# A bank of products goes from two engines to VectorE alone, and one load moves up Pool's queue

## The chip, the cores and the metric

The kernel runs on one core of one Trainium2 chip. The metric is the device time of one execution in microseconds. A core has five engines that run side by side, each through its own instructions in program order: TensorE (matrix products into PSUM), VectorE, ScalarE, Pool (GpSimd) and SyncE, which here only issues transfers. Sixteen DMA engines move the data that SyncE, Pool and, at the end, ScalarE ask for.

## The reference

Two layers stand one behind the other: a global filter in the frequency domain, then a feed-forward net.

```python
# x: (8, 3008, 256); filt_r, filt_i: (1505, 256)
X = np.fft.rfft(x, axis=1)
Y = X * (filt_r + 1j * filt_i)[None, :, :]
y = np.fft.irfft(Y, n=3008, axis=1)
# tokens: 8 * 3008 = 24064; w_in: (256, 2048); w_out: (2048, 256)
h = y.reshape(24064, 256) @ w_in
g = np.maximum(0.01 * h, h)
out = g @ w_out
```

## The kernel before

The transform of 3008 points is split as 94 x 32 and done with matrix products in fp16. For each batch there are four stages on TensorE: stage 1 (94 points; `s1`), stage 2 (32 points with the twiddle factors; `s2`), whose result is multiplied by the filter, and the two inverse stages (`sa` and `sb`). Between stages the data must be turned round. For batches 1 to 7 this goes through DRAM: SyncE stores (`dz1`, `dz2`, lines 259 and 329) and reloads (lines 266 and 273). The result stands in `yt`, and from there the net takes chunks of 512 tokens, 47 in all: `moe1` (line 516) makes `h` in two wide PSUM tiles and ScalarE writes `g`; the second layer follows one chunk later, in the first three chunks by plain products with `w_out` (`plain`, line 641) and later by a scheme of seven products (line 580).

Everything is issued in a fixed order. For batches 1 to 7 and the net, a planner puts each step at a due time on one time line and hands the steps out in that order. For batch 0 the order is written by hand, in the string `FIRST`. Batch 0 is turned round on VectorE (`t1`, `t2`), and nothing of the net can begin before it is through. A step of `FIRST` is a name and its arguments; `hf` is a half of the 256 channels, `c` the first column of the frequency index, `n` the number of columns, `i` the real or the imaginary part, `b` the bank:

- `s2p hf c n i b`: the matmuls of stage 2 for `n` columns, into bank b0 to b2 (512 wide: `pf0` to `pf2`) or b3, b4 (1024 wide: `ph0`, `ph1`).
- `s2d hf c n i`: VectorE multiplies the whole bank by the filter and writes `prods` (line 400, in `times_filter`).
- `s2a hf c n i`: ScalarE copies four columns of a bank to one of six `spare` tiles in SBUF (line 417); `s2m hf c 4 i`: Pool multiplies that copy by the filter (line 400).
- `s2h hf c n i`: VectorE multiplies four columns of a bank whose other four go through ScalarE and Pool.
- `sap`, `sae`: the first inverse stage and its evacuation by ScalarE (lines 427 and 430); `sap hf c b` needs the products of its four columns for both `i`.
- `t2`, `sbp`, `sbe`: turning, the last stage, and its evacuation to `yt`.
- `x 0`, `x 1`: Pool issues the loads of the first and the second half of batch 1's input (line 191; each 768 KB as it lands, cast from fp32 to fp16 on the way); `w_out`: Pool issues the load of the second layer's weights (line 463; 1024 KB as it lands, cast too).

Pool computes and issues loads through one queue, in order. The loads that it has issued before, for batch 0, the filter, the constants and `w_in`, go through the same DMA queue.

The part of batch 1's work in the planner that matters here: its 16 stage-1 groups (line 254) are put between the first layer's products from the start of the net on, their results go to `dz1` in eight stores by SyncE (line 259), four reloads follow (line 266), and then stage 2 (line 303). The second layer's first product stands behind the first layer's 16 steps of chunk 0.

Of the kernel before, what the change touches and what calls it, by code (L numbers as in the profile page):

```python
# [75 lines left out]
def kernel(  # L76
# [9 lines left out]
    nc = tc.nc  # L86
    B, N, D = x.shape
# [264 lines left out]
    act, dve = nc.scalar.copy, nc.vector.tensor_copy  # L352
# [6 lines left out]
    held, spare = {}, [scrp.tile([P, 4, DH], FP32, tag=f"p{i // 2 + 1}", name=f"spare{i}") for i in range(6)]  # L359
# [39 lines left out]
    def times_filter(eng, hf, c, n, i, x):  # L399
        eng.tensor_tensor(prods[hf][:, i, ds(c, n), :], x, fa_sb[:, ds(c, n), ts(hf, DH)], AL.mult)  # L400
# [1 line left out]
    def s2d(hf, c, n, i):  # L402
        times_filter(nc.vector, hf, c, n, i, held.pop(("s2", hf, c, i)))

    def four_of(hf, c, n, i):

        at_c = c if ("s2", hf, c, i) in held else c - 4
        key = ("s2", hf, at_c, i)
        return (held.pop(key) if c - at_c == n - 4 else held[key])[:, ds(c - at_c, 4), :]

    def s2h(hf, c, n, i):
        times_filter(nc.vector, hf, c, 4, i, four_of(hf, c, n, i))

    def s2a(hf, c, n, i):

        held["xf", hf, c, i] = xf = spare.pop(0)
        act(xf[:], four_of(hf, c, n, i))

    def s2m(hf, c, n, i):
        xf = held.pop(("xf", hf, c, i))  # L420
# [44 lines left out]
    def round_x(n0, n, e):  # L465
# [10 lines left out]
        s2a 1 16 8 0, s2p 0 4 4 0 b1, s2p 1 16 8 1 b3, s2d 0 4 4 0, s2a 1 20 8 0, sap 0 8 b2, s2d 0 4 4 1,  # L476
        s2a 1 16 8 1, s2a 1 20 8 1, s2m 0 12 4 0, s2p 0 16 8 1 b4, sap 0 0 b1, s2p 1 0 8 1 b3, s2m 0 12 4 1,
        sap 0 12 b0, s2m 1 20 8 0, sae 0 8 A, s2d 0 16 8 1, sae 0 0 A, s2p 1 8 8 1 b4, sap 0 4 b2, s2d 1 0 8 1,
        sap 0 16 b1, sae 0 12 A, s2p 1 8 8 0 b3, sap 0 20 b0, s2a 1 8 8 1, s2h 1 12 8 1, s2m 1 20 8 1,
        s2m 1 8 8 1, sae 0 4 A, s2d 1 8 8 0, s2p 1 0 8 0 b4, sae 0 16 A, sap 1 20 b2, s2d 1 0 8 0, sap 1 12 b1,  # L480
        sae 0 20 A, sap 1 8 b0, s2m 1 16 8 0, sae 1 20 A, s2m 1 16 8 1, x 0, x 1, w_out, sae 1 12 A, sae 1 8 A,
        sap 1 16 b3, sae 1 16 A, sap 1 4 b2, t2 1, sae 1 4 A, sap 1 0 b4, t2 0, sae 1 0 A, warm 4, sbp 0 1 b1,
        sbp 0 4 b0, sbp 0 0 b3, sbp 0 3 b2, t2 3, sbe 0 1 A, sbe 0 4 A, sbe 0 0 A, sbp 0 2 b4, sbp 0 7 b1,
        sbp 0 6 b0, t2 2, sbe 0 2 A, sbe 0 7 A, sbp 0 5 b3, sbp 1 0 b4, sbp 1 1 b1, sbe 0 6 A, sbe 0 5 A,
        sbe 1 1 A, sbe 0 3 D, sbe 1 0 D
    """
    steps = dict(s1p=s1p, s1e=s1e, t1=t1, s2p=s2p, s2d=s2d, s2h=s2h, s2a=s2a, s2m=s2m, sap=sap, sae=sae, t2=t2,
                 sbp=sbp, sbe=sbe, x=load_x, w_out=load_w_out, xc=round_x, warm=keep_warm)
    for step in FIRST.split(","):
        what, *args = step.split()  # L490
# [210 lines left out]
    while queue:  # L701
        time, n, stage, b, g, f = heapq.heappop(queue)
# [62 lines left out]
```

## Time and profile before

| what | before |
|---|---|
| three runs, us | 752.94, 753.91, 754.14 (median 753.91) |
| the profiled execution, us | 754.14 |
| its span, first to last instruction, us | 752.3 |
| mean granted clock of TensorE | 0.996 |
| busy: TensorE, ScalarE, VectorE, Pool | 98%, 74%, 66%, 22% |
| DMA: mean over the span | 151 GB/s |
| DMA share in the windows 22:28 us, 28:30 us, 30:50 us | 0.95 to 1.11, 0.38 and 0.08, 0.53 to 1.39 |

The span is the time from the first to the last instruction that the profiler recorded; what lies around it is 1.84 us. A row of a group of instructions names the line, the engine, the operation, the tiles written and read, how often, busy time and the mean of one. "Idle before" is the time that an engine stood still before an instruction, with what ended it. A DMA share of 1.00 means that on average all sixteen engines were busy; it can read over 1. The granted clock of TensorE is a share of its full speed.

### The profile page before, as it was taken

To read this page: it belongs to the slowest core of one execution; us is meant where nothing else is said; L and a number is where in the kernel's file an instruction comes from. 1 tells how busy PE (TensorE), PEld (TensorE's weight loads), DVE (VectorE), ACT (ScalarE), POOL (GpSimd) and SP (SyncE) were. 2 spreads that over 40 slices of the span, in tenths; PEclk is the share of its full clock that TensorE was granted. 3 is DMA by queue.
4 is the path that set the end of the run, shared out by engine and by line. 5 is a ranking of instruction groups with operands and counts; after the bars stand their busy time and mean duration, and the time that the engine had idled before them with its cause. 6 is when DMAs were issued, how large, how long until landed. Compare 5 with 4: busy or idle time off the path is not lost.

```text
span 752.3 us, 19411 instructions
## 1 busy us (share of the span) xinstructions
PE 740.2 (98%) x8017; PEld 529.1 (70%) x8017; DVE 498.9 (66%) x684; ACT 559.8 (74%) x756; POOL 169.1 (22%) x172
## 2 busy tenths in 40 slices
PE   9989999999999999999999999999999999999997
PEld 3546667767777777877678777787777777777776
DVE  6867555677767766667667766776677676465565
ACT  4755797788887777787778777877777777767662
POOL 6602430342222321221133222212212210000000
PEclk9999999999999999999999999999999999999999
DMA  9996798887886568565676566544454333211012
GB/s 204 201 226 178 167 216 233 211 184 194 223 204 160 138 180 214 132 155 148 184 185 166 151 171 169 139 135 127 141 163 122 106 100 103 61 54 54 29 47 67
DMA packets 119560, 113.64 MB, mean 151 GB/s; under 512 B 16352, under 2 KB 92768, under 8 KB 119280
## 3 DMA queue, kind: packets, MB, share of 16 engines
q1 hardware_dynamic: 104128, 94.66, 42.8%
q0 software_dynamic: 15056, 17.49, 16.0%
q8 instruction: 62, 1.02, 0.6%
q10 hardware_dynamic: 288, 0.26, 0.1%
q14 instruction: 26, 0.21, 0.1%
HBM read 57.51 MB, written 50.33 MB: 143 GB/s over the span
## 4 chain that ended last, share of the span: by engine, by line
PE 89%; DMA 7%; POOL 1%; DVE 1%; issue 1%; ACT 0%; SPq 0%; POOLq 0%; DVEq 0%; ACTq 0%
PE ph L516 41%; PE po_ps L580 18%; PE pf L580 18%; PE pf L254 3%; PE pf L346 3%; DMA w_out_sb<-in_moe_w_out_dram 3%; PE pf L303 2%; PE pf L325 2%; PE po_ps L641 1%; PE pf L641 1%; DMA f_sb<-fwd_const 1%; DMA fa_sb<-in_filt_i_dram 1%; DMA p_b_g<-p_b_g 1%; DMA dz<-big 1%; POOL prod L400 1%
## 5 line engine op out<-in xcount | busy, mean ns | idle before, releaser
L521 ACT ACTIVATE gt_c<-ph 128x1024 f16<-128x1024 f32 x376 | 385.6, 1026 | 139.7 <-PE ph L516 129.0
L516 PE MATMUL ph<-yt,w_in_sb 128*128 128x512 f16 (+7 forms) x1728 | 447.8, 352 | 0.2
L580 PEld LDWEIGHTS <-gt_c 128*128 128x128 f16 x2800 | 202.2, 98 | 91.3 <-issue 0.2
L318 POOL TENSOR_TENSOR y_b_g<-p_b_g,p_b_g 128x512 f16<-128x512 f32 x84 | 118.1, 1407 | 418.8 <-DMA p_b_g<-p_b_g 219.1
L580 PEld LDWEIGHTS <-big 128*128 128x128 f16 x2128 | 151.3, 98 | 61.6 <-issue 0.2
L516 PEld LDWEIGHTS <-w_in_sb 128*128 128x128 f16 x1728 | 137.6, 98 | 20.0 <-issue 0.5
L312 DVE TENSOR_TENSOR p_b_g<-pf,fb_sb 128x512 f32<-128x512 f32 x78 | 53.7, 689 | 32.6 <-PE pf L303 19.4
L580 PE MATMUL po_ps<-wt_sb,gt_c 128*128 128x128 f16 x704 | 70.0, 219 | 0.0
L580 PE MATMUL pf<-wt_sb,gt_c 128*128 128x128 f16 x688 | 68.4, 219 | 0.0
L580 PE MATMUL pf<-w_out_sb,gt_c 128*128 128x128 f16 x720 | 67.9, 219 | 0.0
L580 PE MATMUL po_ps<-wt_sb,big 128*128 128x128 f16 x720 | 67.4, 219 | 0.0
L580 PE MATMUL pf<-wt_sb,big 128*128 128x128 f16 x704 | 67.2, 219 | 0.0
L580 PE MATMUL po_ps<-w_out_sb,gt_c 128*128 128x128 f16 x688 | 66.0, 219 | 0.0
L257 ACT CAST big<-pf 128x512 f16<-128x512 f32 x98 | 57.1, 588 | 11.9 <-PE pf L254 10.5
L336 ACT CAST yt<-pf 128x376 f16<-128x376 f32 x120 | 56.3, 472 | 10.8 <-PE pf L346 7.9
L315 DVE TENSOR_TENSOR p_b_g<-pf,fa_sb 128x512 f32<-128x512 f32 x84 | 57.3, 682 | 0.2
L553 DVE TENSOR_TENSOR big<-gt_c 128x2048 f16<-128x2048 f16 (+1 forms) x46 | 56.8, 1236 | 0.1
L553 DVE TENSOR_TENSOR big<-big,gt_c 128x2048 f16<-128x2048 f16 (+1 forms) x45 | 55.2, 1226 | 0.1
L553 DVE TENSOR_TENSOR gt_c<-gt_c 128x2048 f16<-128x2048 f16 x43 | 54.4, 1266 | 1.0
L553 DVE TENSOR_TENSOR big<-gt_c,big 128x2048 f16<-128x2048 f16 (+1 forms) x45 | 54.1, 1202 | 0.0
L327 ACT CAST big<-pf 128x512 f16<-128x512 f32 x84 | 49.0, 584 | 4.9 <-PE pf L325 3.0
L254 PE MATMUL pf<-x_sb,small_sb 94*128 94x512 f16 x109 | 41.8, 384 | 0.1
(91 smaller groups left out, 625.8 us busy)
## 6 DMA issues: line engine op xcount, KB each, us to landing
dz<-big SPq DMA_DIRECT2D x98, 256.0 KB
p_b_g<-p_b_g SPq DMA_DIRECT2D x156, 128.0 KB
out_dram<-ost_c_h SPq DMA_DIRECT2D x118, 128.0 KB
big<-dz SPq DMA_DIRECT2D x42, 256.0 KB
big<-dz SPq DMA_DIRECT2D x56, 192.0 KB
x_sb<-in_x_dram POOLq DMA_DIRECT2D x40, 192.0 KB, 4.5
x_sb<-in_x_dram POOLq DMA_DIRECT2D x2, 768.0 KB, 8.2
w_in_sb<-in_moe_w_in_dram POOLq DMA_DIRECT2D x1, 1024.0 KB, 13.1
```

The costliest lines, as they stand in the source:

```text
L254: nc.tensor.matmul(ps, fwd1[:N1], x_sb[:N1, ds(2 * g, 2), :], start=True, stop=True)
L257: copy(st[:, ds(2 * (g % 2), 2), :], ps)
L312: nc.vector.tensor_tensor(p2[:], ps, fb, AL.mult)
L315: nc.vector.tensor_tensor(p1[:], ps, fa, AL.mult)
L318: ("y", b, g), lambda: nc.gpsimd.tensor_tensor(y1[:], p1[:], p3[:], AL.add)))
L327: nc.scalar.copy(st2[h % 4][:, ds(2 * (g % 2), 2), :], ps)
L336: copy(yv, ps.rearrange("p c a -> p a c"))
L346: nc.tensor.matmul(ps[:, j, :], z2[h % 4][:K4, j, ts(dt, P)], i1_sb[:K4, 4 * h + j, :], start=True, stop=True)
L516: nc.tensor.matmul(ph[:, j, ds(t - ci * CH, e - t)], w_in_sb[:, dt, ts(ct, P)], yt[:, dt, ds(t % N, e - t)], start=(dt == 0), stop=(dt == ...
L521: nc.scalar.activation(gts[ci][:, ds(2 * g, 2), :], ph, AF.Lrelu)
L553: nc.vector.tensor_tensor(*(v[:, ds(c0, n)] for v in (o, i0, i1)), op)
L580: nc.tensor.matmul(po[:, t], a()[:, c, ts(t, P)], w[:, c, :], start=(c == 0), stop=(c == NCH - 1))
```

## The change

In `FIRST`, the eight columns 8 to 15 of half 1, part 1 (bank b4) were split: columns 8 to 11 went through ScalarE and Pool (`s2a 1 8 8 1`, `s2m 1 8 8 1`), and VectorE took columns 12 to 15 (`s2h 1 12 8 1`). After the change VectorE takes the whole bank (`s2d 1 8 8 1`), in the same place of its queue. The step `s2h`, now without use, and its helper are taken out. Further, `x 0` is written before `s2m 1 16 8 0`, and `x 1` and `w_out` stay behind `s2m 1 16 8 1`; on Pool's queue the issue of `x 0` thus stands ahead of the last two products and no longer behind them. All the rest of the string is the same, with line breaks moved.

```diff
-    def four_of(hf, c, n, i):
-
-        at_c = c if ("s2", hf, c, i) in held else c - 4
-        key = ("s2", hf, at_c, i)
-        return (held.pop(key) if c - at_c == n - 4 else held[key])[:, ds(c - at_c, 4), :]
-
-    def s2h(hf, c, n, i):
-        times_filter(nc.vector, hf, c, 4, i, four_of(hf, c, n, i))
-
     def s2a(hf, c, n, i):
 
+        at_c = c if ("s2", hf, c, i) in held else c - 4
         held["xf", hf, c, i] = xf = spare.pop(0)
-        act(xf[:], four_of(hf, c, n, i))
+        key = ("s2", hf, at_c, i)
+        act(xf[:], (held.pop(key) if c - at_c == n - 4 else held[key])[:, ds(c - at_c, 4), :])
...
-        sap 0 16 b1, sae 0 12 A, s2p 1 8 8 0 b3, sap 0 20 b0, s2a 1 8 8 1, s2h 1 12 8 1, s2m 1 20 8 1,
-        s2m 1 8 8 1, sae 0 4 A, s2d 1 8 8 0, s2p 1 0 8 0 b4, sae 0 16 A, sap 1 20 b2, s2d 1 0 8 0, sap 1 12 b1,
-        sae 0 20 A, sap 1 8 b0, s2m 1 16 8 0, sae 1 20 A, s2m 1 16 8 1, x 0, x 1, w_out, sae 1 12 A, sae 1 8 A,
+        sap 0 16 b1, sae 0 12 A, s2p 1 8 8 0 b3, sap 0 20 b0, s2d 1 8 8 1, s2m 1 20 8 1, sae 0 4 A,
+        s2d 1 8 8 0, s2p 1 0 8 0 b4, sae 0 16 A, sap 1 20 b2, s2d 1 0 8 0, sap 1 12 b1, sae 0 20 A, sap 1 8 b0,
+        x 0, s2m 1 16 8 0, sae 1 20 A, s2m 1 16 8 1, x 1, w_out, sae 1 12 A, sae 1 8 A, sap 1 16 b3,
```

More of the change, by code (lines that the diff above doesn't have):

```diff
@@ L403, in s2d, with s2a @@
         times_filter(nc.vector, hf, c, n, i, held.pop(("s2", hf, c, i)))
-    def four_of(hf, c, n, i):
+    def s2a(hf, c, n, i):
         at_c = c if ("s2", hf, c, i) in held else c - 4
+        held["xf", hf, c, i] = xf = spare.pop(0)
         key = ("s2", hf, at_c, i)
-        return (held.pop(key) if c - at_c == n - 4 else held[key])[:, ds(c - at_c, 4), :]
-    def s2h(hf, c, n, i):
-        times_filter(nc.vector, hf, c, 4, i, four_of(hf, c, n, i))
-    def s2a(hf, c, n, i):
-        held["xf", hf, c, i] = xf = spare.pop(0)
-        act(xf[:], four_of(hf, c, n, i))
+        act(xf[:], (held.pop(key) if c - at_c == n - 4 else held[key])[:, ds(c - at_c, 4), :])
     def s2m(hf, c, n, i):
@@ L478 @@
         sap 0 12 b0, s2m 1 20 8 0, sae 0 8 A, s2d 0 16 8 1, sae 0 0 A, s2p 1 8 8 1 b4, sap 0 4 b2, s2d 1 0 8 1,
-        sap 0 16 b1, sae 0 12 A, s2p 1 8 8 0 b3, sap 0 20 b0, s2a 1 8 8 1, s2h 1 12 8 1, s2m 1 20 8 1,
-        s2m 1 8 8 1, sae 0 4 A, s2d 1 8 8 0, s2p 1 0 8 0 b4, sae 0 16 A, sap 1 20 b2, s2d 1 0 8 0, sap 1 12 b1,
-        sae 0 20 A, sap 1 8 b0, s2m 1 16 8 0, sae 1 20 A, s2m 1 16 8 1, x 0, x 1, w_out, sae 1 12 A, sae 1 8 A,
[L482 to L485, printed above, removed]
+        sap 0 16 b1, sae 0 12 A, s2p 1 8 8 0 b3, sap 0 20 b0, s2d 1 8 8 1, s2m 1 20 8 1, sae 0 4 A,
+        s2d 1 8 8 0, s2p 1 0 8 0 b4, sae 0 16 A, sap 1 20 b2, s2d 1 0 8 0, sap 1 12 b1, sae 0 20 A, sap 1 8 b0,
+        x 0, s2m 1 16 8 0, sae 1 20 A, s2m 1 16 8 1, x 1, w_out, sae 1 12 A, sae 1 8 A, sap 1 16 b3,
+        sae 1 16 A, sap 1 4 b2, t2 1, sae 1 4 A, sap 1 0 b4, t2 0, sae 1 0 A, warm 4, sbp 0 1 b1, sbp 0 4 b0,
+        sbp 0 0 b3, sbp 0 3 b2, t2 3, sbe 0 1 A, sbe 0 4 A, sbe 0 0 A, sbp 0 2 b4, sbp 0 7 b1, sbp 0 6 b0,
+        t2 2, sbe 0 2 A, sbe 0 7 A, sbp 0 5 b3, sbp 1 0 b4, sbp 1 1 b1, sbe 0 6 A, sbe 0 5 A, sbe 1 1 A,
+        sbe 0 3 D, sbe 1 0 D
     """
-    steps = dict(s1p=s1p, s1e=s1e, t1=t1, s2p=s2p, s2d=s2d, s2h=s2h, s2a=s2a, s2m=s2m, sap=sap, sae=sae, t2=t2,
+    steps = dict(s1p=s1p, s1e=s1e, t1=t1, s2p=s2p, s2d=s2d, s2a=s2a, s2m=s2m, sap=sap, sae=sae, t2=t2,
                  sbp=sbp, sbe=sbe, x=load_x, w_out=load_w_out, xc=round_x, warm=keep_warm)
```

## The prediction

> **What bounds the kernel now.** I read the page first, then TensorE's waits, then the chain of work that ended last over the first 60 us, then Pool and VectorE in order of time, then one-microsecond windows.
>
> ```profile
> span 752.3 us, 19411 instructions
> ...
> PE 740.2 (98%) x8017; PEld 529.1 (70%) x8017; DVE 498.9 (66%) x684; ACT 559.8 (74%) x756; POOL 169.1 (22%) x172
> ```
>
> TensorE is busy 740.2 of 752.3 us. So a change is worth what it does to TensorE's few idle microseconds, or to its clock. The waits of TensorE in the first 75 us (us in total, times, longest):
>
> ```profile
> PE po_ps L641 <- DMA w_out_sb<-in_moe_w_out_dram: 3.3, 1, 3.3
> ...
> PE pf L303 <- DVE p_b_g L315: 0.9, 1, 0.9
> ...
> PE ph L427 <- POOL prod L400: 0.2, 1, 0.2
> ```
>
> The largest wait of the kernel is the first product of the second layer (L641) waiting for its weights. The chain of waits says why they are late (start, length, what):
>
> ```profile
> 26.80 2.28 POOL prod L400 x2
> 29.08 1.06 POOL x_sb L191 x2
> 30.14 18.87 DMA w_out_sb<-in_moe_w_out_dram
> 49.01 0.05 issue
> 49.05 0.61 PE po_ps L641 x4
> ```
>
> Pool issues the load of `w_out` only after its products and the two loads of batch 1's `x`; it lands 18.87 us later. TensorE's last matmul before it ended at 45.79 (49.05 less the 3.26 us of idle that the timeline gives). Pool, then VectorE, in order of time:
>
> ```profile
> 23.04 2.29 POOL L400 TENSOR_TENSOR prod<-spare,fa_sb 128x512 f16<-128x512 f32 x2 [0.55 <-DMA fa_sb<-in_filt_i_dram]
> 25.68 3.40 POOL L400 TENSOR_TENSOR prod<-spare,fa_sb 128x512 f16<-128x512 f32 x3 [0.35 <-ACT spare L417]
> 29.02 1.13 POOL L191 DMA_DIRECT2D x_sb<-in_x_dram  x2
> ```
>
> ```profile
> 22.82 2.35 DVE L400 TENSOR_TENSOR prod<-ph,fa_sb 128x1024 f16<-128x1024 f32 x2
> 25.64 3.11 DVE L400 TENSOR_TENSOR prod<-ph,fa_sb 128x512 f16<-128x512 f32 x3 [0.46 <-ACT spare L417]
> 28.66 2.36 DVE L436 STREAM_TRANSPOSE big<-big 128x1024 f32<-128x1024 f32 x2
> ```
>
> Windows (the last three figures are granted clock, DMA share, GB/s):
>
> ```profile
> 28.00:29.00 1.00, 0.93 (x5) 0.29 (x4) 1.00 (x2) 1.00 (x3) 1.00 (x1) 1.00 0.38 74
> 29.00:30.00 1.00, 0.87 (x5) 0.39 (x5) 1.00 (x2) 0.88 (x2) 1.00 (x3) 1.00 0.08 20
> 34.00:35.00 1.00, 0.82 (x13) 0.47 (x9) 0.55 (x1) 0.81 (x3) 0.00 (x0) 1.00 0.99 205
> 47.00:48.00 1.00, 0.00 (x0) 0.00 (x0) 0.00 (x0) 0.00 (x0) 0.00 (x0) 1.00 1.11 290
> 51.00:52.00 1.00, 1.00 (x11) 0.55 (x10) 0.00 (x0) 1.00 (x2) 0.00 (x0) 0.50 1.13 344
> ```
>
> Three things are to be seen. At 29 to 30 the DMA engines are nearly idle, though 2.6 MB of loads are about to be asked for. At 47 all five engines stand still. At 51 TensorE runs at half clock: the half-microsecond windows show 0.72 at 50.0, 0.50 from 50.5 to 53.5, 0.87 at 53.5, then 1.00. So the wait costs twice: 3.26 us idle, and 0.5 x (0.28 + 6 x 0.50 + 0.13) = 1.70 us of lost clock.
>
> **The change, part by part.** Four columns of one bank change hands: ScalarE loses one copy (`s2a 1 8 8 1`), Pool one product (`s2m 1 8 8 1`), VectorE's 512-wide product becomes 1024 wide, and on Pool's queue the issue of `x 0` moves ahead of the last two products. The instruction orders of TensorE and SyncE are the same; only the wait of one matmul (`sap 1 8`) on Pool goes.
>
> *VectorE.* Now the 512-wide product starts 0.46 us late, because ScalarE still reads the same bank, and 3.11 us later all three are done. Without the copy it starts when VectorE is free, at about 25.18 (22.82 + 2.35). The bank is full by then, TensorE's last of its matmuls being at 24.94. Three products at the pitch of the row (2.35 / 2 = 1.17) end at 28.69 instead of 28.66: +0.03, nothing. If that 0.46 had not been there, the extra 1.17 - 0.62 = 0.55 would have shown in the transposes.
>
> *ScalarE* loses 0.59 us at 25.02; TensorE runs back to back there, so I count nothing. *TensorE:* the 0.2 us wait for Pool goes, since Pool ends its last product earlier (below). ScalarE's last evacuation (now 30.54 to 31.16) then ends some 0.2 earlier, and the third transpose, which waits 0.16 for it, starts at about 31.08 instead of 31.19. The first layer starts 0.11 earlier.
>
> *Pool.* From 25.33, the end of the second row: one issue of x (1.13 / 2, at most the 0.60 of the dearer one) to 25.93, two products (2 x 1.13) to 28.20, the other issue (0.53) to 28.73, then `w_out`: 1.41 earlier than 30.14. Each x issue is one DMA of 768 KB; the waits of `x 0` (VectorE's cast, stage-1 matmuls) were met by 13 us. Behind it wait two products, which end at 28.20 instead of 29.08, so nobody is later.
>
> *When `w_out` lands.* Late bound: only the issue shift counts, 49.01 - 1.41 = 47.60. Early bound: transfers in this queue follow one another, and there is a hole to fill. The bytes before `x 0` are through at about 28.4 (DMA share 0.38 in the window 28 to 29); x's first bytes come at 30.0. In the windows from 30.0 to 38.6 1.58 MB moved, the two halves of x; so `w_out` began at 38.6, and 1.05 MB to about 48.5 is 106 kB/us, beside SyncE's stores and a load from 37.6 on. With `x 0` asked for at 25.33 its bytes follow at 28.4: 1.57 MB at 205 kB/us end at 36.1. SyncE's first store is issued at 37.59, so `w_out` runs alone to about 38.2 (430 kB), then 619 kB at 106 kB/us: 44.0, and 0.5 to landing, 44.5. The two bounds are 44.5 and 47.6; I take 44.5, because its rows are this very queue.
>
> That is 1.3 us ahead of 45.7, when TensorE asks. So the stall goes: 3.26. The clock loss follows the stall; after the 0.95 us wait at 70 us the clock stays 1.00, so without a stall I count 1.70 back. Bounds of the clock part: 0 to 1.70.
>
> *A rule that speaks against the move.* Pool's issue at 38.37 took 0.90 where the one before took 0.52, and ended at 39.27, just after VectorE's L674, fp16 in SBUF, which ran from 38.20 to 39.16. The Trainium skill ("SBUF — State Buffer", on the "DVE blocks DMA" trap) says that Pool cannot write descriptors while VectorE runs a two-port mode; if that took hold of the new place until 28.69, `x 0` would be out at 29.3 and `w_out` at 32.1, and the sum would stay at 754.1. The same page says that an operation with one operand in SBUF does not contend, and here the products of both engines ran side by side at 1.13 and 1.17. I cost the new place at 0.57 us, the row of the same issue, and nothing more.
>
> *The sum.* 0.11 + 3.26 + 1.70 = 5.07. The profiled execution took 754.14 with a span of 752.3, 1.84 around it: 749.07. That execution is the slowest of the three, 0.23 above the median 753.91, so 748.8 to 749.1 is meant; I say 748.9. Does the rest keep it? After 49 us TensorE's idle is below 2 us up to the tail, and SyncE's stores and reloads are tied to TensorE's own progress, so they move along.
>
> **The rivals.**
> *Part of the wait stays.* `w_out` lands at 47.60: the stall is 1.85 instead of 3.26 and the early start of the layer is lost in it. With the clock kept 754.14 - 1.41 - 1.70 = 751.0; with the clock lost as now 752.7. For it: SyncE's queue competes with an unknown share. Against: the hole at 28.4 to 30. The row is that 3.26 us of idle halves the clock and 0.95 does not. The Trainium skill ("TensorE: Matmul & The Clock Gate", Part 1) says that it takes an idle window of about 3.4 us, free-running; the 3.26 here is already shorter, and by that rule 1.85 would give the 751.0.
>
> *Nothing moves.* The queue is bound by bytes and not by issues, and the hole is only landing time: `w_out` at 49.0, 754.1. Against: 20 GB/s at 29 to 30.
>
> *The debt comes due at batch 1's reload: slower.* TensorE's first L303 (64.72) would come at 59.65. Its operand is loaded by SyncE's L266, issued at 60.63 and used 4.09 later, after eight stores (L259), the last issued at 55.80. DMA is full until 54.3. If the backlog still ends there and the last store then takes 6.03 us, as this queue's p_b_g transfer on the chain at 194.09 does, the operand is there at 54.3 + 6.03 + 4.09 = 64.4: a stall of 4.8, and 1.70 of clock again, 749.07 + 6.5 = 755.5 or more. It decides against the change from 63.0 on (59.65 + 5.07 - 1.70). For it: DMA is saturated from 38 to 54. Against: share 0.03 at 55 to 56, so the backlog ends before the last store, and it ends sooner when the hole is filled.
>
> **How the numbers follow.** Stall gone, 748.9: 0.67. Part stays, clock kept, 751.0: 0.14; clock lost, 752.7: 0.06. Nothing moves, 754.1: 0.03. Slower, 755.5: 0.10. About 0.2%, 1.5 us, is what a measurement can tell here. Faster: 0.67 + 0.14 = 0.81; same: 0.06 + 0.03 = 0.09; slower: 0.10. The range goes from 747.8 (the lowest of the runs lies 1.0 under the median, and the front may give 0.1) to 751.5 (the second case and half a microsecond); 0.19 is left out.
>
> **What will show it.** `x 0` issued at about 25.4, `w_out` at 28.7, no DMA hole at 28 to 30; `w_out` landed by 45; TensorE busy through 45 to 50 at clock 1.00; three 1024-wide VectorE products ending at 28.7; the first L303 at about 59.7 without a wait. It is wrong if `w_out` lands after 46, or if another wait of some microseconds appears between 50 and 70.

## The result

The changed kernel takes 748.94 us (median of four runs, 748.77 to 749.92), the kernel before beside it 754.02 (752.94 to 754.99): the ratio is 0.9936, with a 95% interval of 0.9918 to 0.9953. The profiled execution took 749.05 with a span of 747.3; the one before had 754.14 and 752.3.

The page of the changed kernel, its first lines:

```profile
span 747.3 us, 19408 instructions
...
PE 738.1 (99%) x8017; PEld 528.8 (71%) x8017; DVE 504.8 (68%) x684; ACT 559.2 (75%) x755; POOL 165.0 (22%) x171
```

TensorE's busy time fell by 2.1 us and the span by 5.0, with 8017 matmuls both times: what went is idle time and slow matmuls, not work. Pool in order of time (start, length, engine, line, what):

```profile
22.91 2.28 POOL L400 TENSOR_TENSOR prod<-spare,fa_sb 128x512 f16<-128x512 f32 x2 [0.48 <-DMA fa_sb<-in_filt_i_dram]
25.13 0.60 POOL L191 DMA_DIRECT2D x_sb<-in_x_dram  x1
25.75 2.29 POOL L400 TENSOR_TENSOR prod<-spare,fa_sb 128x512 f16<-128x512 f32 x2
27.98 0.57 POOL L191 DMA_DIRECT2D x_sb<-in_x_dram  x1
28.55 1.18 POOL L456 DMA_DIRECT2D w_out_sb<-in_moe_w_out_dram  x1
```

`x 0` is issued at 25.13 and `w_out` at 28.55; the trace gives 14.8 us to the landing of `w_out`, 43.35, where it was 49.01. The same windows as before (the last three figures are granted clock, DMA share, GB/s):

```profile
28.00:29.00 1.00, 1.00 (x5) 0.44 (x6) 1.00 (x2) 0.99 (x2) 1.00 (x3) 1.00 1.16 238
29.00:30.00 1.00, 1.00 (x6) 0.49 (x5) 1.00 (x2) 1.00 (x3) 0.73 (x1) 1.00 1.00 209
34.00:35.00 1.00, 0.77 (x15) 0.46 (x12) 0.63 (x2) 0.95 (x3) 0.00 (x0) 1.00 1.05 221
47.00:48.00 1.00, 1.00 (x14) 0.65 (x13) 0.09 (x1) 1.00 (x2) 0.00 (x0) 1.00 1.14 357
51.00:52.00 1.00, 1.00 (x13) 0.67 (x10) 1.00 (x3) 0.29 (x1) 0.00 (x0) 1.00 0.40 121
```

The hole in the DMA queue at 28 to 30 is filled (1.16 and 1.00, where it was 0.38 and 0.08), TensorE works through the stretch where all engines stood, and the clock at 51 is 1.00 instead of 0.50. TensorE itself, in order of time:

```profile
45.11 0.59 PE L509 MATMUL ph<-yt,w_in_sb 128*128 128x512 f16 x2
45.54 0.60 PE L634 MATMUL po_ps<-w_out_sb,gt_c 128*128 128x256 f16 x4
...
59.71 0.38 PE L303 MATMUL pf<-big,f_sb 128*128 128x256 f16 x2
```

(Line 634 is the line 641 of before.) The second layer's first product comes at 45.54, right behind the first layer and with no wait; before it came at 49.05. The first matmul of batch 1's stage 2 (L303) comes at 59.71 instead of 64.72. So 3.51 us are won up to the first of these two points, and 14.17 instead of 15.67 us between them win another 1.50: 5.01 in all. From the second point to the end both executions take the same, 687.6 us.

### The profile page after: what moved, and what is told of

Read it like the earlier page. It is cut to its first block, busy times and chain, and to the rows that moved or that the text cites. A ratio compares the mean times of both kernels' runs of the same rounds, so it can differ in the third digit from the quotient of the medians.

```text
span 747.3 us, 19408 instructions
## 1 busy us (share of the span) xinstructions
PE 738.1 (99%) x8017; PEld 528.8 (71%) x8017; DVE 504.8 (68%) x684; ACT 559.2 (75%) x755; POOL 165.0 (22%) x171
## 4 chain that ended last, share of the span: by engine, by line
PE 92%; DMA 4%; DVE 2%; POOL 0%; ACT 0%; issue 0%; SPq 0%; POOLq 0%; DVEq 0%
PE ph L509 42%; PE po_ps L573 18%; PE pf L573 18%; PE pf L254 3%; PE pf L346 3%; PE pf L303 2%; PE pf L325 2%; DMA p_b_g<-p_b_g 2%; PE pf L634 1%; PE po_ps L634 1%; DMA f_sb<-fwd_const 1%; DMA x_sb<-in_x_dram 1%; DVE big L546 0%; POOL y_b_g L318 0%; ACT yt L336 0%; PE pf L437 0%
## 5 line engine op out<-in xcount | busy, mean ns | idle before, releaser
L318 POOL TENSOR_TENSOR y_b_g<-p_b_g,p_b_g 128x512 f16<-128x512 f32 x84 | 115.1, 1372 | 417.8 <-DMA p_b_g<-p_b_g 295.8
L546 DVE TENSOR_TENSOR big<-gt_c 128x2048 f16<-128x2048 f16 (+1 forms) x46 | 59.1, 1284 | 0.1
L546 DVE TENSOR_TENSOR gt_c<-gt_c 128x2048 f16<-128x2048 f16 x43 | 56.1, 1306 | 1.0
L546 DVE TENSOR_TENSOR big<-gt_c,big 128x2048 f16<-128x2048 f16 (+1 forms) x45 | 56.3, 1251 | 0.0
```

Of the source, the lines that this page charges most:

```text
L318: ("y", b, g), lambda: nc.gpsimd.tensor_tensor(y1[:], p1[:], p3[:], AL.add)))
L546: nc.vector.tensor_tensor(*(v[:, ds(c0, n)] for v in (o, i0, i1)), op)
```

## The experiments

Times beside each other are of one chip; the kernel before had a median of 753.19 beside the first four kernels, 752.88 beside the next four and 754.05 beside the last.

**1. The early `x 0` alone** (`e1_x0_alone`): the kernel before, whose bank stays split between VectorE and Pool.

```diff
-        s2m 1 8 8 1, ...
+        x 0, s2m 1 8 8 1, ...
-        ... s2m 1 16 8 1, x 0, x 1, w_out, ...
+        ... s2m 1 16 8 1, x 1, w_out, ...
```

> The kernel before, with only the issue of x 0 moved ahead of Pool's last three products; the split bank stays. My theory, that an early x fills the hole in the DMA queue: w_out is issued at about 29.9, hardly earlier than 30.14, but it lands before 45 and the time is 749.0. Rival, that the issue time of w_out counts and the dropped Pool product made it: w_out lands at about 48.8 and the time is 753.8.

It took 749.15 (748.42 to 749.45), ratio 0.9935 (0.9918 to 0.9952). Pool, in order of time:

```profile
24.86 0.60 POOL L191 DMA_DIRECT2D x_sb<-in_x_dram  x1
25.79 3.39 POOL L400 TENSOR_TENSOR prod<-spare,fa_sb 128x512 f16<-128x512 f32 x3 [0.33 <-ACT spare L417]
29.13 0.57 POOL L191 DMA_DIRECT2D x_sb<-in_x_dram  x1
29.69 1.18 POOL L463 DMA_DIRECT2D w_out_sb<-in_moe_w_out_dram  x1
```

Here `w_out` is issued only 0.45 us earlier than before, and 1.14 later than in the changed kernel; it lands after 14.0 us, at 43.7, and TensorE does not wait. The rival that counts the issue of `w_out` (753.8) falls.

**2. The whole bank to VectorE alone** (`e2_bank_alone`): the changed kernel, with `x 0` again beside `x 1`.

```diff
-        x 0, s2m 1 16 8 0, sae 1 20 A, s2m 1 16 8 1, x 1, w_out, ...
+        s2m 1 16 8 0, sae 1 20 A, s2m 1 16 8 1, x 0, x 1, w_out, ...
```

> The changed kernel, with x 0 put back behind Pool's last product, beside x 1; VectorE keeps the whole bank. Theory of the filled hole: x 0 is issued at 27.6, its bytes begin at about 28.6, w_out lands at about 43.7 and the time is 749.1, so that either half of the change is enough. Rival, that the place of x 0 is what counts: w_out lands after 46 and the time is above 750.5.

It took 749.4 (748.34 to 749.87), ratio 0.9936 (0.9915 to 0.9957). Pool, then TensorE, then two windows:

```profile
27.21 1.12 POOL L191 DMA_DIRECT2D x_sb<-in_x_dram  x2
28.32 1.18 POOL L456 DMA_DIRECT2D w_out_sb<-in_moe_w_out_dram  x1
```

```profile
46.23 0.61 PE L634 MATMUL po_ps<-w_out_sb,gt_c 128*128 128x256 f16 x4 [0.96 <-DMA w_out_sb<-in_moe_w_out_dram]
```

```profile
28.00:29.00 1.00, 1.00 (x6) 0.45 (x5) 1.00 (x2) 1.00 (x3) 1.00 (x2) 1.00 1.11 139
29.00:30.00 1.00, 1.00 (x6) 0.49 (x5) 1.00 (x2) 1.00 (x3) 0.51 (x1) 1.00 0.72 119
```

The two runs together decide between the issue of `w_out` and the queue ahead of it. Of the three kernels this one issues `w_out` first (28.32, against 28.55 and 29.69) and lands it last (46.2, against 43.35 and 43.7); it is the one that issues `x 0` last, at 27.21, and whose windows at 28 to 30 still move only 139 and 119 GB/s. The bytes fit: from 28 to 32 us the DMA engines move 324 kB in the kernel before, 660 here, 848 in run 1 and 888 in the changed kernel, and `w_out` lands 2.8, 5.3 and 5.7 us earlier than before, about one microsecond for each 100 to 120 kB. What counts is when `x 0` begins to use the idle DMA engines.

The landing was expected at 43.7, 2.5 us too early. It came where the rival had it (after 46), and a stall of 0.96 is left; the clock stayed at 1.00 through it. The time is that of the theory, within 0.3 us, and this is in part luck: in the profiled execution (749.63) the first layer began at 34.19, 0.43 before that of the changed kernel, which hides half of the stall, and that start varies from one execution to the next (34.23 in another profile of the changed kernel). By the medians, either half of the change gives nearly all of its gain.

**3. More bytes ahead of `w_out`** (`e3_more_bytes`): the changed kernel, with a load into a tile that nothing reads.

```diff
+    junk = cpool.tile([P, 1536], FP16, name="junk")
     def load_w_out():
+        nc.gpsimd.dma_start(junk[:], moe_w_in[0:P, 0:1536])
```

> The changed kernel, with one more load of 384 KB (as it lands; it is used by nothing) on Pool's queue between x 1 and w_out. At 106 to 205 kB/us that makes w_out 1.9 to 3.7 us later than its 43.35: it lands between 45.3 and 47.1, and TensorE stalls 0 to 1.6 us. If a partial stall keeps the clock, the time is at most 750.6; if the clock falls as in the kernel before, up to 752.1.

The landing was missed by 1.0 us at least: 48.1. The added load lands at 39.3, after SyncE's first store (issued at 37.44), so `w_out` now runs wholly beside SyncE's transfers. The median is 755.11, and the ten runs spread from 749.68 to 758.19 (ratio to before 1.0007, 0.9981 to 1.0033). Two of them, at 749.68 and 749.89, are nearly as fast as the changed kernel; the five slowest take 755.44 to 758.19, more than was expected, and no trace shows what they paid for. The profiled run took 753.19. TensorE's wait (line 637 of this kernel is the line 634 of the changed one) and the windows behind it:

```profile
48.14 0.86 PE L637 MATMUL po_ps<-w_out_sb,gt_c 128*128 128x256 f16 x4 [2.50 <-DMA w_out_sb<-in_moe_w_out_dram]
```

```profile
48.00:49.00 1.00, 0.86 (x5) 0.67 (x6) 0.00 (x0) 0.00 (x0) 0.00 (x0) 0.68 1.03 335
49.00:50.00 1.00, 1.00 (x4) 0.30 (x2) 0.53 (x1) 0.00 (x0) 0.00 (x0) 0.50 1.12 326
50.00:51.00 1.00, 1.00 (x8) 0.45 (x8) 0.16 (x1) 0.62 (x1) 0.00 (x0) 0.50 1.12 328
51.00:52.00 1.00, 1.00 (x11) 0.58 (x10) 0.00 (x0) 0.88 (x2) 0.00 (x0) 0.61 1.12 332
```

A stall of 2.50 us is enough to halve the clock; one of 0.96 (run 2) was not. In windows of 0.1 us the half clock begins at 48.36 and ends 3.41 us later; in the kernel before it begins at 50.22, more than a microsecond after the stall, and lasts 3.41 us too. From the product at 48.14 to the first L303 (63.80) it is 15.66, as in the kernel before, so this execution pays 2.60 for the later product and 1.49 for the clock. The late `w_out` of before is made again in a kernel that has all the rest of the change, and in the profiled execution the time returns.

**4. and 5. The clock without the early load** (`e4_warm_in_stall`, `e5_half_warm`): matmuls on zeros in the stall of the kernel before, 13 of them, and 7 in `e5_half_warm`.

```diff
     gts, osts, phs = {}, {}, {}
+    at(SL + 0.005, lambda: keep_warm(13))
```

> The kernel before, with 13 matmuls on zeros (13 x 0.216 = 2.8 us) put on TensorE right before the second layer's first product, where it stands still. If the half clock after the stall comes from the stall's idleness, the clock stays at 1.00 from 50 to 54 while w_out lands at 49.0 as before, and the time falls by 1.5 to 1.7, to 752.4. Rival, that the clock falls for another reason (a fixed time, the load of the DMA engines): half clock as before and 754.0.

> The kernel before, with 7 matmuls on zeros (1.5 us) in the place where e4_warm_in_stall has 13, so that none of them can outlast the wait for w_out. The first theory: the clock is worth 1.5 us wherever the stall loses it; with 1.5 of 3.3 us filled, 1.8 us of idleness remain, the clock stays at 1.00, and the first L303 comes 1.5 us sooner after the second layer's first product than in the kernel before (15.67 us there, 14.17 in the changed one). The time is then 752.0 to 752.5. Rival, from e4: what is won ahead of 60 us is lost again in a wait of TensorE for the reload of the next stage at 112 us (1.7 us there), and the time is 753 to 754 though the clock stays.

> e4_warm_in_stall a second time, for its trace. If the 1.7 us wait for the reload at 112 us (L346 on the load of dz2) belongs to this kernel, it is there again; if it is chance in the DMA queue, it is under 0.5 us here, and the time is below 752.5.

The clock stayed at 1.00 after the stall in all three profiles (two of `e4`, one of `e5`), with `w_out` landing at 47.9, 49.1 and 48.0. From the first product to the first L303 it was 14.16, 14.16 and 14.16 us: the idleness of the stall is what halves the clock. But the medians hardly moved: 753.54 for 13 matmuls (ratio 1.0005, 0.9990 to 1.0020), 1.1 us above the forecast, and 752.48 for seven (0.9991, 0.9975 to 1.0008), as forecast but only 0.4 below the kernel before beside it. Two things eat the gain. The 13 matmuls last until 48.26, beyond the landing of `w_out` in the first profile. And a later wait opened, by a different amount each time; in TensorE's waits of `e4_warm_in_stall`:

```profile
PE pf L346 <- DMA big<-dz: 1.7, 1, 1.7
```

In `e5_half_warm` it is 0.7. In the second profile of `e4` nothing is to be seen there, but 1.0 us of idleness is spread over the windows from 130 to 210, and the time of 753.91 misses the forecast of less than 752.5. So the wait for the reload of `dz2` does not belong to every execution of this kernel; the last store before it took 6.45 us in the first profile of `e4` and 5.25 in the kernel before.

**6. The same kernels again** (`before_again`, `after_again`).

> The kernel before a second time, for its trace: how far do the landing of w_out (49.0), the clock after it and the wait at 112 us (0.1) vary from one execution to the next? If the stall alone makes the spread of its times (751.6 to 755.1), the time of this run and its stall differ from the first ones by the same amount.

> The changed kernel a second time, for its trace. With 2.2 us between the landing of w_out (43.35) and its first use (45.54) no stall is expected here, and a time within 0.6 us of 748.9.

The kernel before took 755.50 this time, though its stall was nearly the same:

```profile
49.28 1.03 PE L641 MATMUL po_ps<-w_out_sb,gt_c 128*128 128x256 f16 x4 [3.35 <-DMA w_out_sb<-in_moe_w_out_dram]
...
66.23 0.38 PE L303 MATMUL pf<-big,f_sb 128*128 128x256 f16 x2
```

From the product to L303 it is 16.95 here: the clock fell already within the window 48 to 49 (0.77), before the stall was over, and cost 2.78 instead of 1.50. In windows of 0.1 us it is half from 48.53 to 55.36, 6.83 us, twice the 3.41 of the other execution. So it is mainly the clock, and not the stall, that made this pair differ. The 43 runs of the kernel before in these experiments agree: the 11 with a mean clock of 0.999 or 1.000 have a median of 752.42, the 8 with 0.995 or less 755.4. Between these ends the mean says little, because the clock also falls behind the last matmul, where it costs nothing (0.50 at 745 to 747 in the profile of `after_timed`, whose last matmul ends in the window 742 to 743). The changed kernel took 749.03, with 0.3 us of wait at L303 for its operand's reload. All of its 11 runs lie between 748.48 and 749.92, where the kernel before spreads from 751.03 to 756.63.

**7. The next wait** (`e6_copies_to_act`, beside `after_timed`, the changed kernel again): two evacuations of the changed kernel go to ScalarE.

```diff
-        at(REST[g - 10], lambda g=g: late_sb(1, g - 8, (act, dve)[g % 2]))
+        at(REST[g - 10], lambda g=g: late_sb(1, g - 8, act if g == 11 else (act, dve)[g % 2]))
-            nc.vector.tensor_copy(ot[:], po)
+            (act if (ci, tj) == (0, 3) else dve)(ot[:], po)
```

> The changed kernel, with two evacuations before TensorE's last wait of some size (L303 on VectorE's L315, 1.0 us at 65 us) given to ScalarE: a copy to yt at 59.66 (0.55 us on VectorE) and one of the second layer's results at 63.45 (0.41). VectorE's product starts when its bank is full, at 60.0 instead of 60.24, and 0.45 follow: the wait falls from 1.0 to about 0.3 and the time from 748.9 to 748.3. Rival: ScalarE's evacuations of the first layer come later and TensorE waits for them instead, 749 or more.

> The changed kernel once more, for times beside e6_copies_to_act on the same chip: 748.9, within 0.5 us.

It took 748.15 (747.63 to 749.53; ratio to before 0.9924, 0.9903 to 0.9945) and the changed kernel 749.08 (748.48 to 749.26; 0.9933, 0.9915 to 0.9952). TensorE's wait in its profile:

```profile
PE pf L303 <- DVE p_b_g L315: 0.6, 1, 0.6
```

It fell from 1.0 to 0.6 only. The median is 0.9 lower, but the trace shows 0.4 of it, and the profiled execution itself is the slowest of the six (749.53, against 749.13 for the changed kernel's). The ranges of the six runs overlap and so do the intervals of the two ratios: that this version is faster is not shown.

## Why the prediction was right

The forecast was 748.9 and the median 748.94. The mechanism is what the runs show: an early `x 0` fills the hole, `w_out` lands before TensorE asks, and with the stall the lost clock goes too. That the sum is met to 0.1 us (5.07 forecast, 5.01 between the two executions) is in part luck, for its terms are off by up to 0.3 us in both directions, and how much clock the kernel before loses changes from one execution to the next. Step by step:

- *VectorE at nothing:* holds. In run 1, with the split bank, five products to the first transpose take 5.84 us (22.92 to 28.76), in the changed kernel 5.85 (23.08 to 28.93). The two groups of rows in the changed kernel:

```profile
23.08 5.93 DVE L400 TENSOR_TENSOR prod<-ph,fa_sb 128x1024 f16<-128x1024 f32 x5
28.93 3.59 DVE L429 STREAM_TRANSPOSE big<-big 128x1024 f32<-128x1024 f32 x3
```

  The 0.46 us wait for ScalarE in the same bank pays for the wider product, as the prediction had it.
- *0.11 us earlier start of the first layer:* wrong in its place. The first layer begins at 34.62, 0.18 later than before, because VectorE's whole sequence began later (23.08 instead of 22.82), which the change does not touch. In other profiles it begins at 34.23 and 34.65 (changed) and at 34.67 (before), so a gain of 0.11 can't be seen in one pair. Yet TensorE reaches the second layer's first product sooner. In the kernel before, stage 1's first matmul stood at 35.74, just when its `x` landed (29.02 + 6.7); now `x` is there by 33.6 and that matmul comes at 35.65.
- *Landing of `w_out`, 44.5, with bounds 44.5 and 47.6:* it landed at 43.35, outside the bounds, to the safe side. The hole to fill is shown by runs 1 and 2. The stretch alone on the engines was only worked out, and two errors partly cancel in it. `x 1` landed at 37.3; less the prediction's own 0.5 its bytes ended at 36.8 and not at 36.1, so by the same sum `w_out` ran alone for 1.4 us and not for 2.1. Beside SyncE it then moved at some 163 kB/us (an estimate: the 758 kB that are left, from 38.2 to 42.85), and not at 106. The same sum put run 2's landing 2.5 us too early and run 3's 1.0 too early, so one rate beside SyncE is too simple; what sets it stays open. The lead is 1.2 us by the prediction's own figures (45.7 - 44.5), not 1.3; it was 2.2, so nothing hung on it.
- *Stall, 3.26:* 3.51 between the two executions. The idle time that the timeline gives starts at the modelled end of the last matmul; the next one can start 0.16 earlier than that, and the layer's last matmuls begin 0.09 earlier than before (45.11 instead of 45.20).
- *Clock, 1.70:* 1.50 in this pair of traces. It is the term that varies: the bounds of 0 to 1.70 are too narrow, for it is 2.78 in the second execution of the kernel before, and nothing in some by their mean clock of 1.000. Those with the clock kept have a median of 752.42, 3.5 above the changed kernel, as the stall alone would give; no profile of such an execution was taken. The clock's part of the gain is then what the medians of the kernel before (752.88 to 754.05) lie above 752.42, 0.5 to 1.6 us.
- *The rivals.* "Part of the wait stays" came up in run 2 (0.96, clock kept) and run 3 (2.50, clock lost), not in the changed kernel. The bounds of the clock in that case, kept or lost, are now narrower: 0.96 keeps it, 2.50 loses it. The rule of the Trainium skill ("TensorE: Matmul & The Clock Gate", Part 1), that it takes an idle window of about 3.4 us, does not agree with the 2.50 here, and the measurement decides. What the traces do show is how long the half clock lasts: 3.41, 3.41 and 6.83 us. "Nothing moves" fell with the windows at 28 to 30. "The debt comes due at batch 1's reload": the first L303 was put at 59.65 and came at 59.71, with 0.0, 0.3 and 0.0 us of wait for the reload in three profiles. The rule on Pool's descriptors ("SBUF — State Buffer", the "DVE blocks DMA" trap) found nothing in the new place: 0.60 us for the issue of `x 0`, the figure of its old place. VectorE ran products with one operand in PSUM there, so this does not test the rule.

## What to carry to other kernels

A late transfer is not always cured at its own issue. Look at the queue ahead of it: idle DMA engines just before a burst of loads say that the first load of the burst is late, and issuing that one 3.9 us earlier moved the last one's landing by 5.7 us, although the last one's own issue moved by 1.6. And a stall of TensorE of some microseconds is to be priced with the slow matmuls behind it, here 1.5 or 2.8 us on top of 3.5, for 3.41 or 6.83 us of half clock.

## What was not expected of the hardware

- The same stall, 3.26 and 3.35 us, cost 1.50 us of clock in one execution and 2.78 in another, because the half clock lasted 3.41 us in one and 6.83 in the other. It began 1.2 us after the stall in one and 0.75 before its end in the other. A stall of 2.50 us brought 3.41 us of half clock; with 0.96 the clock stayed.
- With 384 KB more ahead of `w_out` ten runs spread over 8.5 us, without them 11 runs over 1.4. Whether it is the landing of `w_out` that varies so much is not shown: in the three profiles of the changed kernel it lands at 43.35, 43.4 and 44.3, and of the kernel with more bytes there is one.
- The reload of `dz2` at about 112 us has hardly any slack: in five profiles of nearly the same order before it, it made TensorE wait between 0 and 1.7 us. What sets the length of the store ahead of it was not tried.
